# One core, attention and two gated MLPs: the keys' sums read from SBUF, the first DMAs in another order, and P^T v, VectorE's weights work and x pieces moved

## The chip, the cores and the metric

The kernel runs on one core of a Trainium2 chip. The metric is the device time of one execution in microseconds; the median of three runs stands for the kernel. One further execution was recorded by the hardware profiler.

## The reference

Attention with a bias, and behind it two gated MLPs, each on the result of the one before. Four batches, 8 heads, 576 positions, 64 numbers per head; the MLPs see 2304 tokens of 512 numbers with a hidden width of 1536.

```python
scores = q @ k.T / sqrt(64)                       # per head, 576 x 576
cum    = cumsum(maximum(s, 0))                    # s: one number per head and position
scores = where(causal, -1e9, scores + minimum(-(cum[:, None] - cum[None, :]), 0))
attn   = softmax(scores);  x = attn @ v           # heads side by side: 2304 x 512
x = (sigmoid(x @ w_gate) * (x @ w_val)) @ w_out   # first MLP
out = ((x @ w_a) * (x @ w_b)) @ w_out2            # second MLP
```

The six weight matrices arrive in 64-bit floating point.

## The kernel before, in words

**Two parts.** `attention()` works through 32 heads; `mlps()` then runs 1536-wide products in phases over the tokens. TensorE computes with values split into a high and a low half, so each product of the MLPs takes three matmuls (L276 to L278). A weight tile of 512 KB of 64-bit numbers is loaded by SyncE's queue, turned into 32-bit values by one ScalarE (L224) and four VectorE steps (L225, L227, L229, L232), and split by ScalarE (L243) and GpSimd (L244). Nine tiles are treated so during attention (L621), three heads apart; there are three raw buffers and one scratch buffer (`u`, `mag`).

**Order.** In attention every operation has an engine, the operations that it depends on, and a priority; `emit(in_order=True)` (L44) writes out, of the operations whose predecessors are written, always the one with the lowest priority. So each engine's stream, and each DMA queue's, is in the order of priorities, and a waiting instruction holds back all behind it on its engine. One head period is `HT = 6.1`; head i's own time is `t0 = HT * i`. Pools with one buffer each tie steps together: PSUM `g` (row scores), `E` and `F` (transposed scores), `t` (the small transpose and the last piece of the transposed scores), `px` (P^T v).

**A head.** q and k of head i come in by `lqk` (L337). ScalarE rounds them to the high halves (`hq1`, `hk1`, L478 and L479), DMAs copy these to the other 64 partitions (`hk2` on ScalarE's queue L480, `hq2` on SyncE's L481), and VectorE subtracts to get the low halves (`lok` L482, `loq` L484). The bias goes into the same matmul as extra rows: the running sums of s, relative to the start of each quarter (`sums`, L411 to L417, in the SBUF tile `rel`: 128 partitions, quarter by quarter, 32 heads each), and selector rows (`sel`, L385 and L386). For heads 0 to 2 the keys' sums (`relk`, L445) and the queries' sums (`relq`, L423) are copied from `rel` in small DMAs; from head 3 on they come from DRAM (`rel`, L488 and L489), where `relk_d` and `relq_d` were stored by L452, L429 and L454.

TensorE then computes the row scores in two groups, `S(i,0)` and `S(i,1)` (L508, the masks L513), VectorE takes the rows' maxima (`mx`, L521), a small transpose (`mT`, L528), a ScalarE copy (`mc`, L530) and a DMA on ScalarE's queue (`md`, L532) put them into the operand as one more row, and the transposed scores `ST` (L545, L546) come out with the maximum subtracted. ScalarE exponentiates (`ex`, L551), GpSimd masks (`cs`, L567), and `pv` (L582) multiplies with v (`lv`, L341 and L342) in two regions: `pv(i,0)` 256 queries, `pv(i,1)` the rest. ScalarE copies the result out (`xc`, L591), and GpSimd scales it (`xm`, L595) by reciprocals that went through DRAM.

**Order within a period**, on TensorE: `S(i+1,1)`, both regions of `pv(i-2)`, `mT(i+1)`, `S(i+2,0)`, `ST(i)`. At the start, 60 matmuls on a constant (`busy`, L364) run before the first scores; heads 0 to 2 have priorities of their own (`first_at`, L498). The first operand of the MLPs, `xs0`, is prepared during attention in four pieces (`x0h` L628 on ScalarE, `x0l` L629 on VectorE). Two further lines are named below: L205 loads a weight tile, L591 also frees the PSUM that the MLPs' first matmul takes.

Of the kernel before, what the change touches and what calls it, by code (L numbers as in the profile page):

```python
# [7 lines left out]
FP32 = mybir.dt.float32  # L8
# [111 lines left out]
def attn_mlp_kernel(  # L120
# [169 lines left out]
    def attention():  # L290
        with ExitStack() as c2:
# [109 lines left out]

            relk_d = pdr.tile([BH, NR, 2, S], FP32, name="relk_d")
            relq_d = pdr.tile([BH, 3, S], FP32, name="relq_d")
# [51 lines left out]
            relst = ["relk", "relz"] + [("rels", c) for c in range(NR)]  # L455

            HT = 6.1
            NBUSY = 60

# [4 lines left out]
            def head(i):  # L464
# [13 lines left out]
                op(("hq1", i), "ACT", 0.65, lambda: nc.scalar.copy(out=q1[up], in_=r[up]), [("lqk", i)] + done, -251 + 4 * i if i < NR2 else t0 - 3 * HT + 5.2)  # L478
                op(("hk1", i), "ACT", 0.65, lambda: nc.scalar.copy(out=k1[up], in_=r[dn]), [("lqk", i)] + done, -251 + 4 * i if i < NR2 else t0 - 3 * HT + 5.2)  # L479
                op(("hk2", i), "ACT", 0.7, lambda: nc.scalar.dma_start(out=f32(k2[dn]), in_=f32(k1[up])), [("hk1", i)] + done2, -250 + 4 * i if i < NR2 else t0 - 2 * HT + 0.05)  # L480
                op(("hq2", i), "SP", 0.5, lambda: nc.sync.dma_start(out=f32(q2[up]), in_=f32(q1[up])), [("hq1", i)] + done2, -250 + 4 * i if i < NR2 else t0 - 2 * HT + 0.1)  # L481
                op(("lok", i), "DVE", 0.9, lambda: nc.vector.tensor_tensor(  # L482
                    out=k2[up], in0=r[dn], in1=f32(k2[dn]), op=ALU.subtract), [("hk2", i)], -150 + 2 * i if i < 2 else t0 - HT + 3.0)
# [101 lines left out]

                op(("pv", i, 0), "PE", 0.65, lambda: pv(0), [("cs", i, 0), ("lv", i)], t0 + 2 * HT + 0.65, acq=pxk)
                op(("pv", i, 1), "PE", 2.1, lambda: pv(1), [("cs", i, e) for e in range(3)] + [("pv", i, 0)], t0 + 2 * HT + 1.3)
# [33 lines left out]
            for e, key in enumerate(order[:len(early) + NRAW]):  # L621
                split = [4 * HT + 1.6, 4 * HT + 4.6] if e < len(early) else [0, 0]
                weights(sc, *key, [("S", 3 * e - 3, 0)], HT * (3 * e - 2), part=None if e < len(early) else 0,
                        at=[0, 2 * HT + 1.2, 2 * HT + 1.9, 2 * HT + 2.5, 3 * HT + 1.9, 4 * HT + 1.9] + split)

            for k in range(KD):
                t0 = HT * (NH - 12 + k)
                op(("x0h", k), "ACT", 0.4, lambda k=k: nc.scalar.copy(out=xs0[:, 0, k], in_=x_sb[:, k, 0:NB]), [("xm", i) for i in range(H)], t0 + 1.7)  # L628
                op(("x0l", k), "DVE", 0.5, lambda k=k: nc.vector.tensor_tensor(  # L629
                    out=xs0[:, 1, k], in0=x_sb[:, k, 0:NB], in1=f32(xs0[:, 0, k]), op=ALU.subtract), [("x0h", k)], t0 + 2.6)  # L630
            sc.emit(in_order=True)
# [205 lines left out]
```

## Time and profile before

| | |
|---|---|
| time, median of 3 runs | 1130.16 us (1128.74 to 1132.54) |
| the profiled execution | 1131.72 us, its span 1130.0 us, mean granted TensorE clock 0.988 |
| busy, share of the span | TensorE matmul 97%, VectorE 60%, ScalarE 33%, GpSimd 27% |
| bytes moved by DMA | 73.98 MB, mean 65 GB/s |

The page of the profile gives these shares for the whole span. A mean hides stages, so the windows view (busy time of every engine in stretches that one chooses), the waits view (who waited for whom, in total) and the timeline (instructions in order of time) are read for the first 46 us, for the rest of attention (to 236 us) and for the MLPs. A granted clock of 1.00 is 2.4 GHz, 0.50 is 1.2 GHz; between the two a stretch holds both.

### The profile page before, as it was taken

How to read it: one execution, taken by the hardware profiler on the slowest of the kernel's cores; microseconds unless marked ns; L12 is line 12 of the kernel's file. 1: busy time of each engine (PE TensorE's matmuls, PEld its weight loads, DVE VectorE, ACT ScalarE, POOL GpSimd, SP SyncE). 2: the span in 40 equal slices, each digit the busy share in tenths (PEclk: the TensorE clock that was granted, in tenths of full speed). 3: DMA queues.
4: the chain of work that ended last, by engine and by line, in shares of the span. 5: the costliest groups of instructions: out<-in, count | busy, mean ns of one | idle time of the engine just before them, and what ended most of it. 6: DMA issues, size and time to landing. Idle time of an engine off the chain costs nothing.

```text
span 1130.0 us, 14690 instructions
## 1 busy us (share of the span) xinstructions
PE 1100.5 (97%) x5492; PEld 922.7 (82%) x5492; DVE 672.8 (60%) x1004; ACT 370.5 (33%) x614; POOL 304.5 (27%) x343
## 2 busy tenths in 40 slices
PE   5899999999999999999999999999999999999998
PEld 4787777888888888878887888888888888888887
DVE  6688788628248635963596359524953695266333
ACT  2566666544135212421241124324421331132110
POOL 3245645473013201320132013202320232022000
PEclk7799999999999999999999999999999999999999
DMA  4466666533003100310021002101210121000111
GB/s 129 118 179 172 174 157 151 134 93 99 1 2 111 57 1 12 101 56 1 19 94 56 1 19 94 56 1 38 87 45 1 38 93 38 1 19 22 54 38 57
DMA packets 69793, 73.98 MB, mean 65 GB/s; under 512 B 28607, under 2 KB 53367, under 8 KB 69722
## 3 DMA queue, kind: packets, MB, share of 16 engines
q1 hardware_dynamic: 66498, 68.08, 20.9%
q10 hardware_dynamic: 2904, 4.81, 1.8%
q8 instruction: 43, 0.70, 0.3%
q14 instruction: 28, 0.23, 0.1%
q0 software_dynamic: 320, 0.16, 0.1%
HBM read 57.65 MB, written 5.60 MB: 56 GB/s over the span
## 4 chain that ended last, share of the span: by engine, by line
PE 84%; DVE 7%; DMA 4%; issue 2%; POOL 2%; ACT 1%; SPq 0%; ACTq 0%; DVEq 0%; POOLq 0%
PE ps L278 24%; PE ps L277 24%; PE ps L276 24%; PE ps_x L582 5%; PE ps_g L508 2%; DVE raw L229 2%; PE ps_e L545 1%; PE ps_e L546 1%; DVE u L227 1%; DVE raw L232 1%; PE ps_g L513 1%; DMA vx<-in_vm_dram 1%; POOL w L244 1%; DVE nm L521 1%; DMA o<-o 1%
## 5 line engine op out<-in xcount | busy, mean ns | idle before, releaser
L276 PE MATMUL ps<-xs,w 128*128 128x512 f32 (+1 forms) x960 | 353.3, 368 | 0.9 <-ACT xt L591 0.9
L277 PE MATMUL ps<-xs,w 128*128 128x512 f32 (+1 forms) x960 | 353.2, 368 | 0.0
L278 PE MATMUL ps<-xs,w 128*128 128x512 f32 (+1 forms) x960 | 353.1, 368 | 0.0
L726 POOL TENSOR_SCALAR h<-hf 128x512 fp32r<-128x512 f32 (+1 forms) x120 | 90.2, 751 | 515.6 <-DVE hf L715 515.6
L715 DVE TENSOR_TENSOR hf<-ps,g 128x512 f32<-128x512 f32 (+1 forms) x120 | 76.3, 636 | 254.4 <-PE ps L278 253.1
L276 PEld LDWEIGHTS ps<-xs,w 128*128 128x128 f32 x960 | 181.0, 189 | 31.2 <-ACT xt L591 1.0
L277 PEld LDWEIGHTS ps<-xs,w 128*128 128x128 f32 x960 | 181.0, 189 | 30.2
L278 PEld LDWEIGHTS ps<-xs,w 128*128 128x128 f32 x960 | 180.9, 188 | 30.0
L711 ACT ACTIVATE g<-ps 128x512 f32<-128x512 f32 (+1 forms) x120 | 66.5, 554 | 400.5 <-PE ps L278 400.3
L244 POOL TENSOR_TENSOR w<-raw,w 128x512 fp32r<-128x512 f32 x72 | 104.9, 1458 | 176.0 <-ACT w L243 170.9
L729 DVE TENSOR_TENSOR h<-hf,h 128x512 fp32r<-128x512 f32 (+1 forms) x120 | 82.0, 684 | 64.0 <-POOL h L726 64.0
L521 DVE TENSOR_REDUCE nm<-ps_g 128x1 f32<-128x512 f32 (+4 forms) x154 | 73.8, 529 | 38.8 <-PE ps_g L513 38.7
L582 PE MATMUL ps_x<-pt,vx 128*128 128x256 f32 (+1 forms) x434 | 92.6, 365 | 1.4 <-DMA vx<-in_vm_dram 1.2
L278 PE MATMUL ps<-h,w 128*128 128x512 f32 (+1 forms) x240 | 88.5, 369 | 1.5 <-POOL w L244 1.5
L277 PE MATMUL ps<-h,w 128*128 128x512 f32 (+1 forms) x240 | 88.5, 369 | 0.3 <-DVE h L729 0.3
L582 PEld LDWEIGHTS ps_x<-pt,vx 128*128 128x128 f32 x434 | 73.8, 191 | 18.1 <-ACT o L478 1.1
L276 PE MATMUL ps<-h,w 128*128 128x512 f32 (+1 forms) x240 | 88.3, 368 | 0.0
L277 PE MATMUL ps<-w,h 128*128 128x512 f32 x216 | 84.2, 390 | 0.5 <-POOL w L244 0.5
L276 PE MATMUL ps<-w,h 128*128 128x512 f32 x216 | 84.1, 390 | 0.0
L278 PE MATMUL ps<-w,h 128*128 128x512 f32 x216 | 84.0, 389 | 0.0
L567 POOL TENSOR_SCALAR_AFFINE_SELECT pt<-pt 128x256 f32<-128x256 f32 (+1 forms) x96 | 51.1, 554 | 115.1 <-ACT pt L551 109.6
L243 ACT CAST w<-raw 128x512 fp32r<-128x512 f32 x72 | 47.2, 658 | 106.3 <-DVE raw L232 106.2
(100 smaller groups left out, 1398.1 us busy)
## 6 DMA issues: line engine op xcount, KB each, us to landing
raw<-in_moe_w_out_dram SPq DMA_DIRECT2D x24, 512.0 KB
r<-in_qk_dram SPq DMA_DIRECT2D x32, 288.0 KB
raw<-in_moe_w_gate_dram SPq DMA_DIRECT2D x12, 512.0 KB
raw<-in_moe_w_val_dram SPq DMA_DIRECT2D x12, 512.0 KB
raw<-in_moe_w_a_dram SPq DMA_DIRECT2D x12, 512.0 KB
raw<-in_moe_w_b_dram SPq DMA_DIRECT2D x12, 512.0 KB
o<-o SPq DMA_DIRECT2D x32, 144.0 KB
o<-o ACTq DMA_DIRECT2D x32, 144.0 KB
```

Of the source, the lines that this page charges most:

```text
L243: ("ACT", 0.53, lambda: nc.scalar.copy(out=wtile(n, m)[:, 0], in_=value())),
L244: ("Pool", 1.23, lambda: nc.gpsimd.tensor_tensor(out=wtile(n, m)[:, 1], in0=value(), in1=f32(wtile(n, m)[:, 0]), op=ALU.subtract)),
L276: nc.tensor.matmul(out=outp, lhsT=wh, rhs=xh, start=(e == 0), stop=False)
L277: nc.tensor.matmul(out=outp, lhsT=wh, rhs=xl, start=False, stop=False)
L278: nc.tensor.matmul(out=outp, lhsT=wl, rhs=xh, start=False, stop=(e == n - 1))
L521: nc.vector.tensor_reduce(out=nm[0:n, c:c + 1], in_=ps[0:n, p0:p0 + nk], axis=AX.X, op=ALU.max)
L567: nc.gpsimd.affine_select(to, to, [[0, 2], [1, n]][2 - w:], ALU.is_ge, 0.0, base=0, channel_multiplier=-1)
L582: nc.tensor.matmul(out=px[:, 256 + a:256 + q1_], lhsT=vx[:, j], rhs=pt[:, p0:p0 + q1_ - a], start=j == 0, stop=j == js[-1])
L711: op(("g", i, c), "ACT", 0.06 + N * 0.00083, lambda c=c, g=g: nc.scalar.activation(out=sc.get("g", (i, c))[:, 0:N], in_=sc.get("ps", g)[:, ...
L715: op(("hf", i, c), "DVE", 0.07 + N * 0.00104, lambda c=c, u=u: nc.vector.tensor_tensor(out=sc.get("hf", (i, c))[:, 0:N], in0=sc.get("ps", ...
L726: op(("hh", i, c), "Pool", 0.245 + N * 0.00083, lambda c=c, src=src: nc.gpsimd.tensor_scalar(sc.get("h", (i, c))[:, 0, 0:N], src(), 1.0, 1 ...
L729: op(("hl", i, c), "DVE", 0.07 + N * 0.00104, lambda c=c, src=src: nc.vector.tensor_tensor(out=sc.get("h", (i, c))[:, 1, 0:N], in0=src(), ...
```

## The change

- `relk_d` and its store are gone. From head 3 on the keys' sums are copied to the operand straight from `rel` in SBUF (four partitions, two rows of 576 each), in the same place of SyncE's order.
- The first DMAs have another order. `relk` and `relq` of head i stand together at -210 + i, ahead of the copies `hk2` and `hq2`, which move from -250 to about -209; head 2's casts move behind head 0's sums, its selectors from -240 to -220. `relq` goes from ScalarE and GpSimd in turn to: heads 0 and 2 the same two queues, head 1 three on GpSimd's and one on SyncE's. `lok` of heads 0 and 1 moves on VectorE from before the maxima to behind `mx(1,0)` and behind `mx(2,0)`.
- `busy` has 62 matmuls, not 60.
- `pv(i,0)` goes from behind `S(i+3,1)` to in front of it (its priority falls by 0.7; the row scores of that head stand at `t0 + 2 HT`).
- VectorE's weights steps go from the middle of a period (+1.9, +2.5, and +1.9 of the two next) to just before a period's start (-0.15), one period later; the first tile a period later again. The ScalarE and GpSimd splits follow.
- The x pieces go from periods 20 to 23 to periods 27 to 31.

```diff
-            relk_d = pdr.tile([BH, NR, 2, S], FP32, name="relk_d")
...
-                op(("sel", j), ..., (-260, -257, -240, -2)[j], lat=2.2)
+                op(("sel", j), ..., (-260, -257, -220, -2)[j], lat=2.2)
...
-                    name, eng = (("Pool", nc.gpsimd), ("ACT", nc.scalar))[c % 2]
-                    op(("relq", i, c), name, ..., -200 + i, lat=2.2)
+                    name, eng = {"P": ("Pool", nc.gpsimd), "A": ("ACT", nc.scalar), "S": ("SP", nc.sync)}[("APAP", "PPPS", "APAP")[i][c]]
+                    op(("relq", i, c), name, ..., -210 + i + 0.05 * (c + 1), lat=2.2)
...
-            op("relk", "SP", 1.2, lambda: nc.sync.dma_start(
-                out=relk_d.rearrange("b c e s -> c b e s"), in_=f32(rel)), ["sums"], -190, lat=2.5)
...
-            NBUSY = 60
+            NBUSY = 62
+            WLATE = HT
...
-                op(("hq1", i), "ACT", ..., -251 + 4 * i if i < NR2 else t0 - 3 * HT + 5.2)
+                op(("hq1", i), "ACT", ..., (-251, -247, -209.7)[i] if i < NR2 else t0 - 3 * HT + 5.2)
-                op(("hk2", i), "ACT", ..., -250 + 4 * i if i < NR2 else t0 - 2 * HT + 0.05)
+                op(("hk2", i), "ACT", ..., (-209.8, -209.6, -207)[i] if i < NR2 else t0 - 2 * HT + 0.05)
-                op(("hq2", i), "SP", ..., -250 + 4 * i if i < NR2 else t0 - 2 * HT + 0.1)
+                op(("hq2", i), "SP", ..., (-208.5, -207.5, -206)[i] if i < NR2 else t0 - 2 * HT + 0.1)
-                    ... [("hk2", i)], -150 + 2 * i if i < 2 else t0 - HT + 3.0)
+                    ... [("hk2", i)], (-8.7, -8.3)[i] if i < 2 else t0 - HT + 3.0)
...
-                    nc.sync.dma_start(out=f32(k1[D:R1]), in_=relk_d[i].rearrange("c e n -> (c e) n"))
+                    nc.sync.dma_start(out=f32(k1[D:R1]), in_=f32(rel[i:NR * BH:BH]))
...
-                op(("pv", i, 0), "PE", 0.65, ..., t0 + 2 * HT + 0.65, acq=pxk)
+                op(("pv", i, 0), "PE", 0.65, ..., t0 + 2 * HT - 0.05, acq=pxk)
...
-                split = [4 * HT + 1.6, 4 * HT + 4.6] if e < len(early) else [0, 0]
-                weights(sc, *key, ..., HT * (3 * e - 2), ...,
-                        at=[0, 2 * HT + 1.2, 2 * HT + 1.9, 2 * HT + 2.5, 3 * HT + 1.9, 4 * HT + 1.9] + split)
+                split = [5 * HT + 0.2, 5 * HT + 3.2] if e < len(early) else [0, 0]
+                weights(sc, *key, ..., HT * (3 * e - 2) + WLATE * (e == 0), ...,
+                        at=[0, 2 * HT + 1.2, 3 * HT - 0.15, 3 * HT - 0.14, 4 * HT - 0.15, 5 * HT - 0.15] + split)
...
-                t0 = HT * (NH - 12 + k)
+                t0 = HT * (NH - 4 + k)
...
-                ... [("x0h", k)], t0 + 2.6)
+                ... [("x0h", k)], t0 - 0.15)
```

## Rows read from the trace of the kernel before

**Rows 1.** Windows: busy us per engine (count), granted clock, DMA share, GB/s.

```profile
13.14:18.93 5.79, 0.01 (x1) 0.03 (x1) 1.30 (x2) 0.37 (x1) 3.98 (x8) 0.69 0.54 114
18.93:30.90 11.97, 7.25 (x28) 4.90 (x28) 6.09 (x13) 0.51 (x2) 0.00 (x0) 0.50 0.41 120
30.90:37.12 6.22, 4.96 (x18) 3.93 (x19) 3.33 (x6) 3.65 (x6) 1.48 (x3) 0.50 0.61 175
37.12:45.65 8.53, 8.53 (x39) 7.08 (x38) 5.52 (x10) 4.00 (x7) 1.62 (x4) 0.67 0.50 122
100.00:236.00 136.00, 128.61 (x772) 106.53 (x770) 100.06 (x179) 82.17 (x155) 72.92 (x93) 1.00 0.61 149
236.00:1130.00 894.00, 888.07 (x4248) 747.99 (x4248) 501.39 (x687) 237.24 (x367) 194.09 (x191) 1.00 0.14 44
```

**Rows 2.** Waits of TensorE to 44 us: us in total, times, longest.

```profile
PE ps_g L508 <- DMA o<-ya_sb: 6.3, 2, 5.8
...
PE ps_e L545 <- DMA o<-mr: 3.9, 1, 3.9
```

**Rows 3.** Timeline, 0 to 42 us: start, us, engine, line, operation [idle before].

```profile
11.64 3.29 POOL L423 DMA_DIRECT2D o<-ya_sb  x6 [5.57 <-DVE ya_sb L417]
...
14.11 4.73 ACTq L423 DMA_DIRECT2D o<-ya_sb  x6
...
14.37 0.75 DVE L482 TENSOR_TENSOR o<-r,o 64x576 fp32r<-64x576 f32 x1 [0.68 <-DMA o<-o]
...
16.65 2.00 SPq L445 DMA_DIRECT2D o<-ya_sb  x3
...
18.70 0.59 SPq L452 DMA_DIRECT2D relk_d<-ya_sb  x1
...
20.51 1.35 DVE L521 TENSOR_REDUCE nm<-ps_g 128x1 f32<-128x512 f32 x3 [5.39 <-PE ps_g L513]
...
21.78 1.07 DVE L521 TENSOR_REDUCE nm<-ps_x 128x1 f32<-128x256 f32 x2
...
23.18 1.35 SPq L337 DMA_DIRECT2D r<-in_qk_dram  x1
...
32.65 0.67 ACT L478 CAST o<-r 64x576 fp32r<-64x576 f32 x1 [0.32 <-DMA r<-in_qk_dram]
...
33.93 1.01 ACT L551 ACTIVATE pt<-ps_e 128x1024 f32<-128x1024 f32 x1
```

**Rows 4.** Waits of SyncE's queue, 10 to 34 us.

```profile
SPq L488 <- DMA relk_d<-ya_sb: 5.7, 1, 5.7
...
SPq L445 <- DMA o<-o: 1.7, 1, 1.7
```

**Rows 5.** Chain of work that ended last, 13 to 47 us: start, us, what.

```profile
24.14 6.71 DMA o<-mr
```

**Rows 6.** Source view of L423, its DMAs on GpSimd, 0 to 45 us.

```profile
DMA to landing us min/median/max: 2.1/2.6/2.9
```

**Rows 7.** Windows, same columns, 27 to 31 us.

```profile
27.00:31.00 4.00, 0.10 (x1) 0.10 (x1) 1.13 (x3) 0.25 (x1) 0.00 (x0) 0.50 0.25 75
```

**Rows 8.** Waits of TensorE, 44 to 235.9 us.

```profile
PE ps_g L508 <- DVE nm L521: 2.6, 3, 1.5
...
PE ps_g L508 <- DMA o<-relk_d: 1.6, 1, 1.6
...
PE ps_x L582 <- DMA vx<-in_vm_dram: 1.2, 3, 0.6
```

**Rows 9.** Timeline of TensorE in an undisturbed period, 88 to 136 us.

```profile
90.28 0.65 PE L508 MATMUL ps_g<-o 128*128 128x256 f32 x3
...
91.07 2.98 PE L582 MATMUL ps_x<-pt,vx 128*128 128x256 f32 x14
```

**Rows 10.** Timeline, 157 to 176 us: one operation of VectorE, one of GpSimd.

```profile
158.46 1.94 DVE L629 TENSOR_TENSOR xs<-x_sb,xs 128x512 fp32r<-128x512 f32 x1 [0.98 <-ACT xs L628]
...
158.42 1.43 POOL L595 TENSOR_TENSOR x_sb<-xt,rb 64x576 f32<-64x576 f32 x1
```

More of the change, by code (lines that the diff above doesn't have):

```diff
@@ L441, in attention @@
             for j in range(NO):
-                op(("sel", j), "SP", 1.3, lambda j=j: selectors(o_t[j]), ["selc", ("ms", j) if 0 < j < 3 else "more"], (-260, -257, -240, -2)[j], lat=2.2)
+                op(("sel", j), "SP", 1.3, lambda j=j: selectors(o_t[j]), ["selc", ("ms", j) if 0 < j < 3 else "more"], (-260, -257, -220, -2)[j], lat=2.2)
             op("sums", "DVE", 2.7, sums, ["s"], -250)
@@ L477, in head @@
                 op(("lv", i), "SP", 0.9, lambda: load_v(i), [("pv", i - 2, 1), ("sel", 1)], t0 + 4.8, lat=3.0)
[L478 to L481, printed above, removed]
+                op(("hq1", i), "ACT", 0.65, lambda: nc.scalar.copy(out=q1[up], in_=r[up]), [("lqk", i)] + done, (-251, -247, -209.7)[i] if i < NR2 else t0 - 3 * HT + 5.2)
+                op(("hk1", i), "ACT", 0.65, lambda: nc.scalar.copy(out=k1[up], in_=r[dn]), [("lqk", i)] + done, (-251, -247, -209.7)[i] if i < NR2 else t0 - 3 * HT + 5.2)
+                op(("hk2", i), "ACT", 0.7, lambda: nc.scalar.dma_start(out=f32(k2[dn]), in_=f32(k1[up])), [("hk1", i)] + done2, (-209.8, -209.6, -207)[i] if i < NR2 else t0 - 2 * HT + 0.05)
+                op(("hq2", i), "SP", 0.5, lambda: nc.sync.dma_start(out=f32(q2[up]), in_=f32(q1[up])), [("hq1", i)] + done2, (-208.5, -207.5, -206)[i] if i < NR2 else t0 - 2 * HT + 0.1)
                 op(("lok", i), "DVE", 0.9, lambda: nc.vector.tensor_tensor(
-                    out=k2[up], in0=r[dn], in1=f32(k2[dn]), op=ALU.subtract), [("hk2", i)], -150 + 2 * i if i < 2 else t0 - HT + 3.0)
+                    out=k2[up], in0=r[dn], in1=f32(k2[dn]), op=ALU.subtract), [("hk2", i)], (-8.7, -8.3)[i] if i < 2 else t0 - HT + 3.0)
                 op(("loq", i), "DVE", 0.9, lambda: nc.vector.tensor_tensor(
@@ L584, in pv @@
                             start=j == 0, stop=j == js[-1])
-                op(("pv", i, 0), "PE", 0.65, lambda: pv(0), [("cs", i, 0), ("lv", i)], t0 + 2 * HT + 0.65, acq=pxk)
+                op(("pv", i, 0), "PE", 0.65, lambda: pv(0), [("cs", i, 0), ("lv", i)], t0 + 2 * HT - 0.05, acq=pxk)
                 op(("pv", i, 1), "PE", 2.1, lambda: pv(1), [("cs", i, e) for e in range(3)] + [("pv", i, 0)], t0 + 2 * HT + 1.3)
@@ L621, in attention @@
             for e, key in enumerate(order[:len(early) + NRAW]):
-                split = [4 * HT + 1.6, 4 * HT + 4.6] if e < len(early) else [0, 0]
-                weights(sc, *key, [("S", 3 * e - 3, 0)], HT * (3 * e - 2), part=None if e < len(early) else 0,
-                        at=[0, 2 * HT + 1.2, 2 * HT + 1.9, 2 * HT + 2.5, 3 * HT + 1.9, 4 * HT + 1.9] + split)
+                split = [5 * HT + 0.2, 5 * HT + 3.2] if e < len(early) else [0, 0]
+                weights(sc, *key, [("S", 3 * e - 3, 0)], HT * (3 * e - 2) + WLATE * (e == 0), part=None if e < len(early) else 0,
+                        at=[0, 2 * HT + 1.2, 3 * HT - 0.15, 3 * HT - 0.14, 4 * HT - 0.15, 5 * HT - 0.15] + split)
             for k in range(KD):
-                t0 = HT * (NH - 12 + k)
-                op(("x0h", k), "ACT", 0.4, lambda k=k: nc.scalar.copy(out=xs0[:, 0, k], in_=x_sb[:, k, 0:NB]), [("xm", i) for i in range(H)], t0 + 1.7)
+                t0 = HT * (NH - 4 + k)
+                op(("x0h", k), "ACT", 0.4, lambda k=k: nc.scalar.copy(out=xs0[:, 0, k], in_=x_sb[:, k, 0:NB]), [("xm", i) for i in range(H)], t0 - HT + 1.7)
                 op(("x0l", k), "DVE", 0.5, lambda k=k: nc.vector.tensor_tensor(
-                    out=xs0[:, 1, k], in0=x_sb[:, k, 0:NB], in1=f32(xs0[:, 0, k]), op=ALU.subtract), [("x0h", k)], t0 + 2.6)
+                    out=xs0[:, 1, k], in0=x_sb[:, k, 0:NB], in1=f32(xs0[:, 0, k]), op=ALU.subtract), [("x0h", k)], t0 - 0.15)
             sc.emit(in_order=True)
```

4 lines of the change are left out of this document (2 added, 2 removed).

## The prediction

> **What bounds the kernel now.** I read first where TensorE, at 97% of the span, isn't busy, since nothing else can be won. The windows view [rows 1] sorts it by stage. The MLPs, from 236 us on, are busy for 888.07 of 894.00 us: TensorE alone bounds them, and they begin when attention ends. The rest of attention, 100 to 236 us, loses 136.00 - 128.61 = 7.4 us. The start loses most: nothing runs from 13.14 to 18.93 us, 4.7 us are idle from 18.93 to 30.90, and from there to 37.12 another 1.3; nearly all of this runs at the lower granted clock (0.50, 1.2 GHz). The clock fell while TensorE was idle (a mean of 0.69 in a stretch of 5.79 us that holds both levels: 2.2 us after its beginning) and came back in the stretch from 37.12 (mean 0.67, so 5.6 us into uninterrupted work).
>
> Then who ends those waits. TensorE waits 5.8 us in one piece for the last sums of head 0, and 3.9 us for head 0's maxima [rows 2]. The first isn't the sums' computing: GpSimd's copies of them start at 11.64 us, when VectorE is done, but SyncE issues its copies of the keys' sums (L445) only at 16.65 [rows 3], behind a wait of 1.7 us for another copy, o<-o [rows 4]. The second isn't the maxima: their DMA is issued at 24.14 us and lands 6.71 us later [rows 5], against 2.1 to 2.9 us for small copies shortly before [rows 6]. In between, at 18.70, the keys' sums are stored to DRAM [rows 3], and head 3's load from there waits 5.7 us for this store [rows 4]. From 27 to 31 us the DMA engines are busy by 0.25 [rows 7], as much as four of sixteen, and head 3's q and k, issued at 23.18, land only when ScalarE's cast begins, at 32.65 [rows 3].
>
> **The store on four engines: row and skill.** The share of 0.25 [rows 7] says that the tail sits on a quarter of the engines. The Trainium skill, "DMA: Bandwidth & Descriptors", section on why a DMA increments its semaphore by 16, says that a DMA uses the largest number of engines up to 16 that divides the slowest dimension of both sides; the store's is NR = 4, and the trace agrees. The same rule speaks against the new loads of keys' sums: four partitions on one side put them on four engines, where eight rows from DRAM went to eight. By it the one wait of 1.6 us for this load [rows 8] could at most double, and the sum would be 1122.1; on the rows alone it stays.
>
> **The change, part by part.** *To head 0's row scores.* The sums end at about 11.5 us as now. SyncE has its selectors out by then, and the keys' sums go at once instead of at 16.65; GpSimd issues its two of head 0 first (six take 3.29 us [rows 3], so the second is issued by 12.2), ScalarE its two by 13 (six take 4.73). With the median landing of 2.6 us [rows 6] the last arrives at 14.8 (bounds 14.3 with 2.1, 15.9 with ScalarE's last and 2.9). So `S(0,0)` starts at 14.8, not 18.93: **-4.1 us**. The two additional matmuls of `busy` lengthen a run of 60 that is over at 13.14 us by 2/60 of at most 13.14, 0.4 us, and end before 14.8; without that cover they'd cost these 0.4.
>
> *From there to the transposed scores of head 0* (now 11.97 us [rows 1]). With the store gone, `md` lands in 2 to 3 us, and VectorE's line of maxima is what is late next: three reductions of group 0 take 1.35, two of group 1 1.07 [rows 3]. In front of `mT(1)`, which precedes `ST(0)` on TensorE, stand 0.9 of scores, 1.35 + 1.07 + 1.35, then `lok` of head 0 (0.75 [rows 3]), which the change puts there, and 1.07; some 0.4 for transpose and signals: 6.9 us, to 21.7. `md(0)`, issued after the first two maxima at 19.0, lands at 21.6, level with this. **-5.1 us**. Bounds: -3.9 if `md` lands late beside the copies `hk2`, `hq2` and the first weight tile; -6 if it lands in 2 us and the scores are short. The weight load isn't moved on SyncE's queue by its later priority: nothing stands there between -12.2 and -6.1.
>
> *To head 3's row scores* (now 6.22 us). Head 3's q and k may be loaded when `lok(0)` has read the buffer, at 20.3 (now they're issued at 23.18). With 3 us (one more than the smallest landing, for 288 KB) ScalarE casts from 23.3, two times 0.67, then exponentiates 1.01 and two smaller pieces (0.8, from their sizes), with a DMA issue of some 0.6 in between (as the store's [rows 3]). The last piece frees `t` for `mT(2)`, at 27.3, and `S(3,0)` starts at 27.6: 5.9 us, **-0.3**. TensorE has nothing from about 24.5 to 27.3. Bounds: +1.5 if that load lands like the copies queued now, -1 if earlier.
>
> *Head 3 to head 4* (now 8.53 us, its first 5.6 at 1.2 GHz). If the idle 2.8 us drop the clock again, the stretch stays as it is: **0**. If the clock holds, it takes one period, 6.0 (scores, 0.65 + 0.14 for group 1, P^T v 2.98 [rows 9]), with 0.4 for the queues to fill: -2.1. The trace has one comparable row: idle from 13.14 us on, the clock fell within 2.2 us. I take the fall.
>
> *P^T v in front.* `S(i+3,1)` waited three times for VectorE's maxima, 2.6 us in total [rows 8]. The x pieces stood there: one took 1.94 us at 158.46 [rows 10]. Without them in those periods, with the weights steps in the gap before the scores of group 1, and with `pv(i,0)` filling 0.65 us, this goes: **-2.6** (bounds 0 and -2.6). In exchange `pv(i,0)` wants v earlier by the length of group 1, 91.07 - 90.28 = 0.79 us [rows 9], and all behind it on TensorE waits: group 1, its maxima, `mT`. Three heads wait for v already (1.2 us in all [rows 8]); each pays 0.79 more: **+2.4** (bounds 0, if the loads fall otherwise, and 4, if two more heads join).
>
> *The remaining parts cost nothing.* The x pieces at periods 27 to 31 lie where no weights step is left; uncovered, one VectorE piece costs up to 1.94 us before the MLPs. The new load of keys' sums stands in the same place of the queue; the wait of 1.6 us for it [rows 8] stays (bounds: gone, or doubled by four engines). The later weights are needed at 236 us at the earliest.
>
> **The sum** against the profiled execution: -4.1 - 5.1 - 0.3 + 0 - 2.6 + 2.4 = -9.7, so 1131.7 - 9.7 = 1122.0. That execution lies 1.6 above the median of the runs shown; against the median 1130.16 the forecast is 1120.5 us.
>
> **Rivals.** *The clock holds* (chance 0.27): `busy` ends nearer the scores, and the idle stretches are shorter than the 5.79 us of now. It saves the 2.1 above: 1118.4 us. Against it stands the idle stretch before `mT(2)`.
>
> *The start wins half* (0.15): the copies to the other partitions and the first weight tile land together behind the sums, `lok(0)` and head 3's casts wait for them, and ScalarE's stream holds back the exponentials. For it: head 3's casts stand ahead of `ex(0,0)`. With 14.8 kept and 5 us lost again: 1125.5 us.
>
> *VectorE collides with GpSimd* (0.08): the weights steps now stand right before the maxima of group 1. The piece of 1.94 us at 158.46 began beside GpSimd's scaling of x, 1.43 us from 158.42 [rows 10]; doing so in each of nine tiles' three slots, with half of them past the slack before `mT` by 0.4 us, costs 13 x 0.4 = 5: also 1125.5. The Trainium skill, "SBUF — State Buffer", on the shared port pair as an exclusive lock, states such blocking of a VectorE operation with two SBUF inputs by a reading GpSimd one; the long piece fits it, the quick ones beside it don't decide.
>
> *The v loads become the bound* (0.05), the slower side: with `pv(i,0)` first, every head waits for v, because its load follows ScalarE's copy-out on SyncE's queue and can't start earlier. Up to 0.79 us on 29 heads is 23 us: 1130.2 - 9.7 - 2.4 + 23 = 1141. It makes the kernel slower from 12.1 / 29 = 0.4 us per head on. Against it: three waits only among 29 heads now.
>
> *The change is off the path* (0.03): no gain at the start arrives, because the weights of the MLPs set their beginning: 1130. Against it: the first matmul of the MLPs follows attention's last copy, not a weight.
>
> **How the numbers follow.** The forecast has the remaining 0.42 and is the likeliest: 1120.5. Its own range, with the bounds of its terms, is 1117 to 1124.5. The range of 8 in 10 must take in the held clock with the v loads costing nothing (1116) and the two cases at 1125.5: 1115.5 to 1126. A measurement of this kernel tells 0.3%, 3.4 us, from no change, so faster means below 1126.8: all of forecast and held clock, most of the two at 1125.5: 0.86. Within: 0.09, from their rest and the fifth. Slower: 0.05, the v loads.
>
> **What would show it.** `S(0,0)` at 14.3 to 15.9 us; no wait of TensorE over 1 us for md at head 0; `ST(0)` at about 21.7; `S(3,0)` near 27.6, `S(4,0)` near 36 (34 with the clock held), and in the windows a granted clock that falls once after 24 us, or not at all. No TensorE wait on L521 near the x pieces; waits on v of 2 to 4 us in all; MLPs of 894 us as before, begun near 226 us. The prediction is wrong if `md(0)` still takes over 4 us (then the store wasn't its cause), if `mT` waits for VectorE in many periods, or if the time won by 45 us is gone by 236.

## The result and the profile after

The changed kernel takes 1120.45 us (median of four runs, 1117.89 to 1122.1), the kernel before, beside it, 1129.86 us: a ratio of 0.9913, 95% interval 0.9898 to 0.9927. The forecast was 1120.5 us. The profiled execution of the changed kernel is its fastest run (1117.89 us, span 1116.2), 2.6 us below the median; that of before (1131.72) lies 1.9 above the 1129.86. So the two profiles differ by 13.8 us where the medians differ by 9.4, and a stage read from one profile is held below against the other kernels that share the same code.

The line numbers of the changed kernel are one lower than before. First the windows, cut at the same events as [rows 1]: the start to `S(0,0)`, to `ST(0)`, to `S(3,0)`, to `S(4,0)`, a late stretch of attention, the MLPs. Columns: busy us of TensorE's matmuls, its weight loads, VectorE, ScalarE and GpSimd (instructions), granted clock, DMA share, GB/s.

```profile
10.50:13.96 3.46, 3.12 (x29) 2.58 (x28) 1.39 (x2) 0.76 (x2) 3.21 (x6) 1.00 0.12 25
13.96:21.83 7.87, 5.02 (x28) 3.15 (x28) 6.77 (x15) 1.09 (x3) 2.76 (x6) 0.84 0.82 206
21.83:27.98 6.15, 4.89 (x19) 3.92 (x19) 2.79 (x5) 3.57 (x6) 0.99 (x3) 0.65 0.61 168
27.98:33.99 6.01, 6.01 (x39) 5.03 (x38) 5.36 (x10) 3.15 (x6) 1.27 (x3) 1.00 0.85 218
100.00:221.95 121.95, 118.46 (x708) 98.35 (x707) 95.50 (x168) 75.34 (x142) 59.77 (x84) 1.00 0.62 151
221.95:1116.00 894.05, 888.10 (x4248) 748.40 (x4248) 501.09 (x687) 237.12 (x367) 194.31 (x191) 1.00 0.14 44
```

The idle 5.79 us of [rows 1] have shrunk to the 0.34 in front of `S(0,0)`, which starts at 13.96; `ST(0)` starts at 21.83 (before 30.90), `S(4,0)` at 33.99 (before 45.65), the MLPs at 221.95 (before 235.99). The MLPs themselves are as long as they were. The two mixed clocks hold one fall and one rise: 0.84 of 7.87 us is 2.5 us at 1.2 GHz at its end, and 0.65 of 6.15 us is 4.3 at its beginning, 6.8 us together; before, it was from 15.4 to 42.7 us.

The steps in the timeline (start, us, engine, line, operation, idle before and what ended it), in order of time:

```profile
10.47 1.18 SPq L444 DMA_DIRECT2D o<-ya_sb  x2
10.75 3.79 POOL L422 DMA_DIRECT2D o<-ya_sb  x7 [4.69 <-DVE ya_sb L416]
13.96 0.70 PE L507 MATMUL ps_g<-o 128*128 128x512 f32 x3 [0.34 <-ACT o L477]
16.45 0.71 PE L507 MATMUL ps_g<-o 128*128 128x512 f32 x3 [0.91 <-DVE nm L520]
17.88 0.79 ACTq L531 DMA_DIRECT2D o<-mr  x1
20.15 0.35 SPq L337 DMA_DIRECT2D r<-in_qk_dram  x1
21.83 0.80 PE L544 MATMUL ps_e<-o 128*128 128x512 f32 x1 [0.80 <-DMA o<-mr]
23.73 0.67 ACT L477 CAST o<-r 64x576 fp32r<-64x576 f32 x1 [2.41 <-DMA r<-in_qk_dram]
27.74 0.27 PE L527 MATMUL ps_t<-idf,nm 128*5 128x128 f32 x1 [1.26 <-DVE nm L520]
27.98 0.70 PE L507 MATMUL ps_g<-o 128*128 128x512 f32 x3
33.99 0.71 PE L507 MATMUL ps_g<-o 128*128 128x512 f32 x3
```

And TensorE's waits after 44 us (us in total, times, longest), against [rows 8]: the maxima (2.6) are gone, and v costs 2.0 instead of 1.2. A head's sums held it twice before, once for the keys' (1.6) and once for the queries' (0.7, the last line, of the kernel before); now they hold it once, for 1.2.

```profile
PE ps_x L581 <- DMA vx<-in_vm_dram: 2.0, 5, 0.6
PE ps_g L507 <- DMA o<-relq_d: 1.2, 1, 1.2
PE ps L276 <- ACT xt L590: 0.8, 1, 0.8
```

```profile
PE ps_g L508 <- DMA o<-relq_d: 0.7, 1, 0.7
```

### The profile page after: what moved, and what is told of

Its sections match the earlier page's. It is cut to its first block, busy times and chain, and to the rows that moved or that the text cites. A ratio compares the mean times of both kernels' runs of the same rounds, so it can differ in the third digit from the quotient of the medians.

```text
span 1116.2 us, 14691 instructions
## 1 busy us (share of the span) xinstructions
PE 1096.7 (98%) x5494; PEld 920.1 (82%) x5494; DVE 676.7 (61%) x1004; ACT 370.4 (33%) x614; POOL 295.0 (26%) x344
## 4 chain that ended last, share of the span: by engine, by line
PE 83%; DVE 6%; DMA 6%; issue 1%; ACT 1%; POOL 1%; SPq 1%; ACTq 0%; DVEq 0%; POOLq 0%
PE ps L278 24%; PE ps L277 24%; PE ps L276 24%; PE ps_x L581 5%; DMA vx<-in_vm_dram 2%; DVE raw L229 2%; PE ps_g L507 2%; DVE u L227 1%; PE ps_e L544 1%; DVE raw L232 1%; PE ps_e L545 1%; DMA o<-o 1%; PE ps_g L512 1%; POOL w L244 1%; DVE h L728 1%
## 5 line engine op out<-in xcount | busy, mean ns | idle before, releaser
L581 PE MATMUL ps_x<-pt,vx 128*128 128x256 f32 (+1 forms) x434 | 99.6, 370 | 2.1 <-DMA vx<-in_vm_dram 2.0
L581 PEld LDWEIGHTS ps_x<-pt,vx 128*128 128x128 f32 x434 | 76.2, 191 | 19.0 <-ACT o L477 1.5
L566 POOL TENSOR_SCALAR_AFFINE_SELECT pt<-pt 128x256 f32<-128x256 f32 (+1 forms) x96 | 40.5, 440 | 113.3 <-ACT pt L550 112.1
```

The lines of the kernel that those rows point to most:

```text
L566: nc.gpsimd.affine_select(to, to, [[0, 2], [1, n]][2 - w:], ALU.is_ge, 0.0, base=0, channel_multiplier=-1)
L581: nc.tensor.matmul(out=px[:, 256 + a:256 + q1_], lhsT=vx[:, j], rhs=pt[:, p0:p0 + q1_ - a], start=j == 0, stop=j == js[-1])
```

## The experiments

Twelve kernels ran. The kernel before had medians from 1129.35 to 1130.94 us beside them, so they are compared by their ratio to it, each with its 95% interval; 0.001 is 1.1 us. Two events place a profile: `S(4,0)`, the end of the start, and the first matmul of the MLPs.

**The start alone.** P^T v, the weights steps and the x pieces are as before.

```diff
-                op(("pv", i, 0), "PE", ..., t0 + 2 * HT - 0.05, acq=pxk)
+                op(("pv", i, 0), "PE", ..., t0 + 2 * HT + 0.65, acq=pxk)
...
-                weights(sc, *key, ..., HT * (3 * e - 2) + WLATE * (e == 0), ...
+                weights(sc, *key, ..., HT * (3 * e - 2), ...
...
-                t0 = HT * (NH - 4 + k)
+                t0 = HT * (NH - 12 + k)
```

> The changed kernel with P^T v, the weights steps and the x pieces back in their places of before; the store is gone, the first DMAs reordered, 62 matmuls in front. My theory (the start carries the gain): head 4's row scores start at 34 to 36 us against 45.65, and the time is 9 to 11 us under the kernel before; the waits for VectorE's maxima of 2.6 us near the x pieces come back. Rival (the start's gain is lost again before 236 us without the later parts): 5 us or less under the kernel before.

Measured: 0.9930 (0.9909 to 0.9952), 1123.45 us; `S(0,0)` at 15.19, `ST(0)` at 24.65, `S(4,0)` at 38.53. That is less than the theory (34 to 36 us, and 9 to 11 us under the kernel before): the medians lie 6.8 us apart. TensorE waits 3.6 us for the maxima later on, as it said. By the ratios the start carries four fifths of the gain (0.0070 of 0.0087).

**The later parts alone**, in the kernel before: the same three edits the other way.

```diff
-                op(("pv", i, 0), "PE", ..., t0 + 2 * HT + 0.65, acq=pxk)
+                op(("pv", i, 0), "PE", ..., t0 + 2 * HT - 0.05, acq=pxk)
...
-                t0 = HT * (NH - 12 + k)
+                t0 = HT * (NH - 4 + k)
```

> The kernel before with P^T v in front, the weights steps and the x pieces as in the changed kernel, and the start untouched. My theory: the waits for maxima (2.6 us) go, the waits for v grow by up to 2.4; the time is 0 to 2.6 us under the kernel before. Rival (most of the gain sits here): 5 us or more under it. Slower rival: the waits for v grow by over 3 us, and the kernel is slower than before.

Measured: 0.9983 (0.9968 to 0.9997), 1128.43 us, 1.8 us under the kernel before beside it, as the theory says. The waits for the maxima are gone, v costs 1.2 us over two heads.

**No store**, in the kernel before: the keys' sums come from SBUF, the order of the first DMAs stays.

```diff
...
-            op("relk", "SP", 1.2, lambda: nc.sync.dma_start(
-                out=relk_d.rearrange("b c e s -> c b e s"), in_=f32(rel)), ["sums"], -190, lat=2.5)
...
-                    nc.sync.dma_start(out=f32(k1[D:R1]), in_=relk_d[i].rearrange("c e n -> (c e) n"))
+                    nc.sync.dma_start(out=f32(k1[D:R1]), in_=f32(rel[i:NR * BH:BH]))
```

> One edit to the kernel before: no store of the keys' sums, the loads from head 3 on read SBUF. My theory (the store alone holds up head 0's maxima and head 3's operands): the DMA of head 0's maxima lands in 2 to 4 us instead of 6.7, the transposed scores of head 0 start at 26.5 to 28 us instead of 30.9, head 0's row scores stay at 18.9; 3.5 to 5.5 us under the kernel before. Rival (the weight load of 512 KB issued beside it holds them up): the DMA still takes over 5 us and the time changes by under 1 us.

Measured: 0.9977 (0.9962 to 0.9993), 1128.24 us. `md(0)` lands 3.97 us after its issue instead of 6.71 [rows 5], TensorE's wait for it falls from 3.9 us [rows 2] to 1.2, and `ST(0)` comes at 27.86 instead of 30.90, but `S(4,0)` only at 42.47, and the medians lie 2.0 us apart: the mechanism held, the gain was smaller than the 3.5 to 5.5 us expected.

**The store in another layout**, in the kernel before: 128 rows outermost (4 quarters of 32 heads) instead of 4 quarters.

```diff
-            relk_d = pdr.tile([BH, NR, 2, S], FP32, name="relk_d")
+            relk_d = pdr.tile([NR * BH, 2, S], FP32, name="relk_d")
...
-                out=relk_d.rearrange("b c e s -> c b e s"), in_=f32(rel)), ["sums"], -190, lat=2.5)
+                out=relk_d, in_=f32(rel)), ["sums"], -190, lat=2.5)
...
-                    nc.sync.dma_start(out=f32(k1[D:R1]), in_=relk_d[i].rearrange("c e n -> (c e) n"))
+                    nc.sync.dma_start(out=f32(k1[D:R1]), in_=relk_d[i:NR * BH:BH])
```

> One edit to the kernel before: the store stays, with the same bytes, but its outer dimension is 128 partitions instead of 4, so that all sixteen engines may share it; the loads from DRAM read it in that layout. If it is the four engines that make it late: landing in 3 to 5 us instead of 11.5, no stretch at a DMA share of 0.25 from 27 to 31 us, and nearly the gain of the kernel without the store (3 to 5 us under the kernel before). If it is the bytes or the write to DRAM: landing above 8 us and under 1 us gained.

Measured: 0.9980 (0.9966 to 0.9995), 1127.74 us: 2.5 us under the kernel before, a little less than expected and about what leaving the store out gives. The store lands 3.6 us after its issue instead of 11.55. In the waits view of SyncE's queue, the 5.7 us of [rows 4] that head 3's load waits for the store become

```profile
SPq L488 <- DMA relk_d<-ya_sb: 0.2, 1, 0.2
```

The bytes are the same; the outermost dimension of the copy differs, and with it the order of the rows in DRAM. That it is the four engines shows in the trace of the kernel before. It holds a landing mark for each of a load's parts, and head 3's q and k have sixteen: twelve are in by 27.07 us, the other four come at 30.36, 30.52, 31.69 and 32.63, each 2.3 to 2.4 us behind one of the store's four (27.98, 28.14, 29.41 and 30.24). With the store in the other layout all sixteen are in by 24.73. So a quarter of the engines held up the store, and with it a part of every load queued behind it, as the prediction read from [rows 7]. The rule of the Trainium skill cited there ("DMA: Bandwidth & Descriptors", the section on why a DMA increments its semaphore by 16) agrees.

**The changed kernel with the store**, in its old layout: the new order, without the new source.

```diff
...
+            op("relk", "SP", 1.2, lambda: nc.sync.dma_start(
+                out=relk_d.rearrange("b c e s -> c b e s"), in_=f32(rel)), ["sums"], -190, lat=2.5)
...
-                    nc.sync.dma_start(out=f32(k1[D:R1]), in_=f32(rel[i:NR * BH:BH]))
+                    nc.sync.dma_start(out=f32(k1[D:R1]), in_=relk_d[i].rearrange("c e n -> (c e) n"))
```

> The changed kernel with its new order of loads, but the head's keys' sums are stored to memory and loaded from there again, as before. Theory (the new order and the missing store are two separate savings that meet at the dynamic mask's first load): S(0,0) still starts at 14 to 15 us, but the first mask load is issued beside the store and lands at about 26 to 28 us, so ST(0) starts at about 28 instead of 21.8 us, S(4,0) comes 2 to 5 us later than in the changed kernel, and the time is 1123 to 1127 us. Rival (the order alone carries the gain): ST(0) stays within 1 us of 21.8 and the time stays at 1120 to 1121.5 us.

Measured: 0.9988 (0.9977 to 0.9999), 1127.56 us. Nearly all of the gain is gone, more than expected, although `S(0,0)` starts at 14.82. Three rows of its timeline:

```profile
26.25 0.79 PE L547 MATMUL ps_e<-o 128*128 128x512 f32 x1 [4.48 <-DMA o<-mr]
32.94 0.67 ACT L480 CAST o<-r 64x576 fp32r<-64x576 f32 x1 [10.87 <-DMA r<-in_qk_dram]
35.86 0.38 PE L530 MATMUL ps_t<-idf,nm 128*5 128x128 f32 x1 [4.89 <-DMA vx<-in_vt_dram]
```

`md(0)`, issued at 18.73 beside the store, lands at 26.21. Worse is the second row: head 3's q and k, issued at 23.73, land at 32.92, and ScalarE waits 10.87 us for them with a cast; the exponentials of head 0 stand behind that cast. The third row's releaser is misread by the view (that load lands at 36.98, later than the matmul): `mT(2)` needs the buffer `t`, which the last exponential reads until 35.81. `S(4,0)` comes at 43.66, two microseconds before [rows 1]'s 45.65.

**The changed kernel with the store in the other layout.**

```diff
...
+            op("relk", "SP", 1.2, lambda: nc.sync.dma_start(
+                out=relk_d, in_=f32(rel)), ["sums"], -190, lat=2.5)
...
-                    nc.sync.dma_start(out=f32(k1[D:R1]), in_=f32(rel[i:NR * BH:BH]))
+                    nc.sync.dma_start(out=f32(k1[D:R1]), in_=relk_d[i:NR * BH:BH])
```

> The changed kernel with the keys' sums stored and loaded again, but stored as 96 rows of one layout, the form that landed in 3.6 instead of 11.5 us when it was put into the kernel before. Theory (the store's slowness on four DMA engines, not the round trip, is what cost 7 us when it was put back): the store lands in 3 to 5 us, the raw rows that ScalarE waited 10.9 us for land before 26 us, S(4,0) is within 2.5 us of the changed kernel's 34.0, and the time is 1120.5 to 1123 us. Rival (the round trip, its bytes and its place on the queue cost as much in any form): 1125 to 1128 us.

(The rows are 128, not 96.) Measured: 0.9951 (0.9932 to 0.9969), 1126.59 us median, though its profiled execution took 1121.65. The store lands in 4.8 us, q and k of head 3 at 25.86, `S(4,0)` at 36.40: in the profile the theory holds, but the median lies in the rival's range, and half of what was lost stays lost. So by ratio the store costs 0.0075 in the new order, of which 0.0037 is its layout and 0.0038 the round trip itself, where it was 0.0023 in the old order (no store) in all. Each of the two parts is uncertain by about 0.002.

**P^T v back behind the scores.**

```diff
-                op(("pv", i, 0), "PE", ..., t0 + 2 * HT - 0.05, acq=pxk)
+                op(("pv", i, 0), "PE", ..., t0 + 2 * HT + 0.65, acq=pxk)
```

> The changed kernel with P^T v's first part put back behind the row scores' group 1. Theory (the maxima waits went with the x pieces and weights steps, and the part of P^T v in front only brings the wait for the v loads earlier): TensorE's wait for v loads falls from 2.0 us to between 0 and 1.2, the maxima waits stay under 1 us in all, the time is 1118.5 to 1120.5 us. Rival (the part of P^T v in front is what removed the waits for the maxima): 2 to 3 us of such waits come back and the time is about 1122 to 1123.5 us.

Measured: 0.9918 (0.9906 to 0.9931), 1119.62 us. The waits for v are gone, 2.6 us of waits for the maxima are back (the theory had said under 1; this part is as the rival says), and the time is that of the changed kernel all the same: a swap of one wait for another of about the same size.

**The x pieces back.**

```diff
-                t0 = HT * (NH - 4 + k)
+                t0 = HT * (NH - 12 + k)
```

> The changed kernel with the eight x pieces put back to the batches where they stood before, on ScalarE and VectorE. Theory (they held up the maxima): TensorE's waits for the maxima in the last third of the attention come back with 1 to 3 us and the time is 1121.5 to 1123.5 us. Rival (the other two moves are enough): no wait for the maxima over 0.5 us in all, 1120 to 1121 us.

Measured: 0.9923 (0.9910 to 0.9936), 1120.74 us, waits for the maxima of 0.4 us. The theory fell: with P^T v in front, the x pieces do not hold up the maxima.

**VectorE's weights steps back.**

```diff
-                split = [5 * HT + 0.2, 5 * HT + 3.2] if e < len(early) else [0, 0]
-                weights(sc, *key, ..., HT * (3 * e - 2) + WLATE * (e == 0), ...
-                        at=[0, 2 * HT + 1.2, 3 * HT - 0.15, 3 * HT - 0.14, 4 * HT - 0.15, 5 * HT - 0.15] + split)
+                split = [4 * HT + 1.6, 4 * HT + 4.6] if e < len(early) else [0, 0]
+                weights(sc, *key, ..., HT * (3 * e - 2), ...
+                        at=[0, 2 * HT + 1.2, 2 * HT + 1.9, 2 * HT + 2.5, 3 * HT + 1.9, 4 * HT + 1.9] + split)
```

> The changed kernel with VectorE's weights steps (and the first weight's steps that WLATE delays) put back to where they stood before. Theory (neither the x pieces nor the part of P^T v brought the maxima waits back when they were put back, so these steps were what held up the maxima): TensorE's waits for the maxima between 45 and 222 us come back with 1.5 to 3 us, and the time is 1121.5 to 1123.5 us. Rival (any two of the three moves are enough): under 1 us of such waits, 1120 to 1121 us.

Measured: 0.9968 (0.9956 to 0.9981), 1127.51 us: 6 us of the gain are lost, three times what the theory said, and not through the maxima (0.2 us). TensorE's waits from 45 us to the MLPs name another:

```profile
PE ps_x L581 <- ACT xt L590: 5.6, 12, 0.5
```

P^T v of a head waits, in twelve heads, for ScalarE's copy of the result of the head before. One such period, all engines:

```profile
125.33 2.26 POOL L566 TENSOR_SCALAR_AFFINE_SELECT pt<-pt 128x256 f32<-128x256 f32 x3 [2.93 <-ACT pt L550]
125.77 0.84 DVE L229 SCALAR_TENSOR_TENSOR raw<-raw,u 128x512 int32<-128x512 int32 x1
126.64 0.85 DVE L481 TENSOR_TENSOR o<-r,o 64x576 fp32r<-64x576 f32 x1
127.67 1.44 POOL L594 TENSOR_TENSOR x_sb<-xt,rb 64x576 f32<-64x576 f32 x1
129.14 0.64 ACT L590 COPY xt<-ps_x 128x576 f32<-128x576 f32 x1 [1.85 <-POOL x_sb L594]
129.83 0.92 PE L581 MATMUL ps_x<-pt,vx 128*128 128x256 f32 x4 [0.50 <-ACT xt L590]
```

From bottom to top: P^T v waits for the copy, the copy for GpSimd's scaling (L594, which frees the copy's target), the scaling stands behind GpSimd's three mask pieces (L566), and these take 2.26 us while VectorE runs a weights step (L229) and `lok` (L481) beside them. The changed kernel at the same place:

```profile
125.54 0.64 DVE L229 SCALAR_TENSOR_TENSOR raw<-raw,u 128x512 int32<-128x512 int32 x1
125.75 1.24 POOL L566 TENSOR_SCALAR_AFFINE_SELECT pt<-pt 128x256 f32<-128x256 f32 x3 [3.24 <-ACT pt L550]
126.96 1.42 POOL L594 TENSOR_TENSOR x_sb<-xt,rb 64x576 f32<-64x576 f32 x1
127.19 1.80 DVE L481 TENSOR_TENSOR o<-r,o 64x576 fp32r<-64x576 f32 x1
```

The mask pieces take 1.24 us, and now `lok` is the longer one, beside the scaling. The groups of GpSimd's masks from 45 to 222 us (xcount | busy us, mean ns of one | idle before; the mean mixes pieces of 128x256 with a smaller one of 64x64), of the kernel before, the changed kernel and this experiment:

```profile
L567 POOL TENSOR_SCALAR_AFFINE_SELECT pt<-pt 128x256 f32<-128x256 f32 (+1 forms) x84 | 46.1, 572 | 85.7 <-ACT pt L551 80.2 <-PE ps_g L513 4.7 <-POOL pt L567 0.2
```

```profile
L566 POOL TENSOR_SCALAR_AFFINE_SELECT pt<-pt 128x256 f32<-128x256 f32 (+1 forms) x87 | 36.6, 439 | 93.9 <-ACT pt L550 93.0
```

```profile
L566 POOL TENSOR_SCALAR_AFFINE_SELECT pt<-pt 128x256 f32<-128x256 f32 (+1 forms) x82 | 50.0, 630 | 81.9 <-ACT pt L550 78.5 <-PE ps_g L512 3.0
```

**The start and the weights steps**, without the other two moves (the edits of P^T v and of the x pieces above, together).

```diff
+                op(("pv", i, 0), "PE", ..., t0 + 2 * HT + 0.65, acq=pxk)
...
+                t0 = HT * (NH - 12 + k)
```

> The change without two of its parts: the start and VectorE's weights steps as in the changed kernel, P^T v's first part and the x pieces as before. Theory (VectorE's weights steps used to run beside GpSimd's masks and lengthen them, 572 ns a piece before, 630 with the weights steps put back, 439 in the changed kernel; moving these steps carries all that the later parts bring): the masks take 430 to 460 ns a piece, ScalarE's copies out of P^T v wait for GpSimd under 20 us in all, TensorE waits for the maxima under 1.5 us, and the time relative to the kernel before is 0.990 to 0.9925, as in the changed kernel. Rival (the weights move only repairs what P^T v in front would cost, and by itself brings nothing): 0.993, as with the start alone, with 3 us or more of waits for the maxima.

Measured: 0.9928 (0.9906 to 0.9950), 1122.16 us. The masks take 430 ns a piece and the copies wait 14.7 us for GpSimd, as the theory says; but the waits for the maxima are 3.9 us, as the rival says, and the time lies between the two and doesn't decide. The moves' worth can be read only in combination: the weights steps' place is worth 6 us with P^T v in front, and nothing measurable without (0.9928 against the start alone, 0.9930). The other way round, P^T v in front and the late x pieces without the weights move (0.9968) lose 4 us against the start alone.

**TensorE's gaps filled.** 35 matmuls on constants that nothing reads, in the gaps of the changed kernel's start.

```diff
...
+            for n, at in ((8, -8.89), (2, -8.71), (6, -8.55), (3, -8.41), (6, 4.1), (10, 9.45)):
+                op(("fill", at), "PE", 0.1 * n, fill(n, ("fill", at)), ["mkb"] + ([("ex", 0, 1)] if at > 5 else []) + [("S", 0, 1)], at, ...)
```

> The changed kernel with 35 matmuls that nothing reads put into TensorE's idle gaps between S(0,1) and mT(2) of the first batch; nothing else moves. Theory (about a third of a microsecond of time goes with each microsecond that TensorE spends at its lower clock level, and the clock falls because of those gaps): the granted clock stays at its upper level from S(0,0) on or falls for under 2 us in place of 6.8 in the profile and 9.0 in the mean of the runs, and the time falls by 1 to 3 us to 1117.5 to 1119.5 us. Rival (the start is bound by loads and by VectorE alone, the clock only follows): the clock is held and the time stays within 0.7 us of 1120.4. Second rival: the fillers stand in front of due matmuls and the time rises by up to 2 us.

Measured: 0.9929 (0.9910 to 0.9949), 1120.95 us. The runs spend 4.9 us at the lower clock in the mean (from each run's mean clock; 9.0 in the changed kernel's), yet nothing is won: the time is the first rival's. The last ten fillers waited 2.1 us for the exponentials that free their buffer and ran 1.25 us in front of `mT(2)`, which came at 28.76 instead of 27.74.

**Only the first 25 fillers**, and P^T v behind (the edit of P^T v above, and against the kernel with all fillers).

```diff
-            for n, at in ((8, -8.89), (2, -8.71), (6, -8.55), (3, -8.41), (6, 4.1), (10, 9.45)):
+            for n, at in ((8, -8.89), (2, -8.71), (6, -8.55), (3, -8.41), (6, 4.1)):
```

> The changed kernel with the first 25 of the 35 filling matmuls (those before mT(2), which waited for the exponentials and ran 1.25 us in front of it, are left out) and with P^T v's first part behind the row scores' group 1. Theory (the lower clock level costs time by itself): at most 5 us at the lower level in the mean of the runs, S(3,0) at 28.0 us or earlier, and 1118 to 1119.3 us, 0.5 to 2 us under the changed kernel. Rival (the clock level of the start only goes with the loads' lateness, and the loads set the time): the same 1119.5 to 1121 us as with all fillers.

Measured: 0.9928 (0.9909 to 0.9948), 1122.68 us; 4.9 us at the lower clock in the mean. The theory fell; the median lies above the rival's range too. The kernel with P^T v behind and no fillers is the one to hold this against (0.9918, its clock low from 19.59 to 26.42 us). With the fillers the clock holds in that stretch, and `S(3,0)`, at 27.81, comes 13.18 us after `S(0,0)` instead of 14.04. That is only 0.86 us sooner, because another path then ends last: head 3's q and k, its casts and the exponentials, for which `mT(2)` waits:

```profile
27.60 0.38 PE L527 MATMUL ps_t<-idf,nm 128*5 128x128 f32 x1 [2.10 <-ACT pt L550]
```

And the clock falls all the same, later, in the period from `S(3,0)` to `S(4,0)`, where TensorE has no gap. That stretch in the kernel with the x pieces back and in this one, against 6.01 us in the changed kernel (at 1.00) and in the one with P^T v behind:

```profile
29.64:37.24 7.60, 7.60 (x38) 6.43 (x38) 5.67 (x10) 3.22 (x6) 1.00 (x3) 0.78 0.45 108
```

```profile
27.81:36.52 8.71, 8.71 (x39) 7.27 (x38) 5.06 (x9) 3.64 (x7) 1.48 (x5) 0.65 0.71 172
```

0.78 of 7.60 us is 3.3 us at 1.2 GHz and costs 1.6; 0.65 of 8.71 is 6.1 and costs 2.7: somewhat under half a microsecond for each, where TensorE is busy throughout. In the changed kernel's profile the lower clock lay from 19.35 to 26.17 us, in stages whose ends are set by `md(0)` and by VectorE's maxima, with waits of 0.80 and 1.26 us at these ends. In that gappy start 6.8 us at the lower clock cost 0.86, about an eighth of a microsecond for each. The fillers did not avoid the fall, they moved it on, in this profile into a stretch that TensorE alone bounds.

## Why the prediction was right

The order of the waits, their causes in the main and the gain came out as forecast: 9.4 us by the medians, where 9.7 were summed. That the median hits 1120.5 to 0.1 us is luck, since several steps are off and partly cancel, and one was right by a wrong cause. Profile against profile:

| step | forecast | profile | what it was |
|---|---|---|---|
| to `S(0,0)` | -4.1 | -5.0 | 13.96 us; 14.43, 14.64, 14.77, 14.84 and 15.19 in the other five profiles with this start, no store and no fillers |
| to `ST(0)` | -5.1 | -4.1 | `md(0)` took 3.9 us, not 2 to 3 |
| to `S(3,0)` | -0.3 | -0.1 | set by the maxima, not by head 3's load |
| to `S(4,0)` | 0 | -2.5 | the clock was back |
| rest of attention | -2.6 + 2.4 | -2.4 | maxima as forecast, v less, the sums' loads 1.1 less |
| MLPs | 0 | +0.2 | 894.25 against 894.01 us |

**To `S(0,0)`** the step held. The profile's extra 0.9 us is not the change's: the load of s, for which VectorE's sums wait, landed at 6.65 us, in the other five at 7.13 to 7.88 (GpSimd's copies start at 10.75 us, against 11.64 in [rows 3]), and in all six `S(0,0)` starts 3.2 us after the first of these copies. The view puts the end of its wait to a cast of ScalarE for head 2, on which it doesn't depend; by the trace's landing marks, the last of head 0's sums, issued by ScalarE at 11.96 us, landed at 13.61. The six starts together have a median of 14.7 us, where 14.8 was forecast.

**To `ST(0)`** the path was named rightly, but its end was `md(0)`, level with the maxima in the forecast: issued at 17.88 us, a microsecond earlier than thought, it landed 3.9 us later, and TensorE waits 0.80 us for it. The result, -4.1, is near the bound of -3.9 that stood for an `md` that lands late. The reason given there, the copies and the first weight tile beside it, isn't shown: without the store, in the old order, `md(0)` takes 3.97 us too, issued at 23.84, when the weight tile has landed (22.11). In the other five profiles with this start it takes 3.88 to 4.85 us, in three of them over 4, which is the prediction's own sign that the store wasn't the cause. The runs with and without the store put it in between, since the store caused a part of the landing: 2.7 of 6.71 us in the old order (3.97 without it), 3.6 of 7.48 in the new (3.91 without it). That a small copy lands here in 2 to 3 us without the store was wrong.

**To `S(3,0)`** the time was right and the cause wrong. Head 3's q and k were cast from 23.73 us (forecast 23.3), but the last exponential freed `t` at 26.66, not 27.3; what ended last was VectorE's maxima of `S(2,1)`, a group that TensorE ran at the lower clock. In the other four profiles with this start and the weights steps or P^T v moved, or the x pieces back, `S(3,0)` comes at 28.47 to 29.64 us, and in the start alone at 30.87, later than the forecast's 27.6.

**To `S(4,0)`** the forecast let the clock fall in the idle stretch after 24 us and charged it to this stretch. In the profile it fell at 19.35, in the gaps between the first scores, was back at 26.17, and the stretch took 6.01 us, the held-clock rival's time (6.0 and 0.4). Which of the two happens differs between executions: 7.60 us with the x pieces back, whose start is the same code. `S(4,0)` came at 33.99, 34.48, 36.27, 36.52 and 37.24 us in these five and at 38.53 in the start alone, on both sides of the forecast's 36.15; the profiled run is the earliest and the fastest; the others of the changed kernel have no profile. What was measured is thus probably a mixture of the forecast and that rival. The sum against the profiled run (1122.0) missed its 1117.89 by 4.1 us: 2.5 for the clock, 2.2 for the rest of attention and 0.9 for the early sums, less 1.4 for later steps that came out slower.

**Rest of attention.** The maxima's 2.6 us went, as forecast, but of the three moves that it gave as causes one suffices. With P^T v in front these waits are 0 to 0.4 us in every kernel (the x pieces or the weights steps back included), with P^T v behind 1.7 to 3.9; there the late x pieces make 1.3 us of difference (2.6 against 3.9, one profile each). v pays 0.8 us more, not 2.4: five heads wait, two more than before, as the upper bound allowed, but each shortly. The waits for the loads of a head's sums, which the forecast let stand, fell from 2.3 us in two to 1.2 in one; but the same loads cost 2.8 us in four waits in the kernel before without its store, and with the x pieces back this one among others:

```profile
PE ps_g L507 <- DMA o<-ya_sb: 2.4, 1, 2.4
```

So whether the doubling that the prediction worked out from the rule of the Trainium skill ("DMA: Bandwidth & Descriptors", the section on why a DMA increments its semaphore by 16) happens there isn't decided. The x pieces' later dates cost nothing measurable, as forecast. The weights steps' move, to which the sum gave no price of its own, is worth 6 us beside P^T v in front.

**The rivals.** VectorE's collision with GpSimd was seen with the wrong sign: the old place of the weights steps is the colliding one, and the price of 5 us that stood for the new place is what the old one costs (6 us) once P^T v stands in front. The mechanism of the start that wins half, casts of head 3 that hold back the exponentials, is what the changed kernel with the store in it shows; there it takes nearly the whole gain. The v loads as the bound and the gain off the path are refuted: 2.0 us of waits, and what is won by `S(4,0)` (11.7 us) is still there at the MLPs (14.0).

**What the forecast did not see** is that the two halves of the start need each other. It added -4.1 for the order and -5.1 for the store as if each stood alone. By ratio the store's removal alone gives 0.0023; the new order with the store gives nothing beyond the later parts (0.9988 against their 0.9983); both give 0.0070. The first wait hides the second: with the order alone the store is issued just when `md(0)` and head 3's q and k must go out.

Open are three things: what besides the store keeps `md(0)` at 3.9 us and more; why the round trip in the fast layout still costs 0.0038 in the median, since its profiled execution is the fastest of its six runs and shows little of it; and what P^T v in front brings at all, since its two halves cancel within the intervals.

## What to carry to other kernels

Where two waits follow each other on one path, price the edits together as well as apart: removing either one here gave a third of what both gave, or nothing. A step that moves one engine's work is judged by who runs beside it at the new place and at the old one, and the price may appear three engines away. Before filling gaps to keep TensorE's clock up, see where the clock would fall instead: each microsecond at the lower level cost about an eighth of one in the start with its gaps, almost half of one in a stretch that TensorE alone bounds.

## What the runs showed of the hardware

A GpSimd mask piece of 128x256 takes 0.41 us when no two-input VectorE operation runs beside it, and 0.64 to 0.75 us when one does (medians of 17 to 39 pieces from 45 to 222 us in the kernels before, changed, and with the weights steps back); spans on GpSimd are rough, but ScalarE's copy and P^T v move with them. The reverse holds too: `lok` takes 0.75 us alone [rows 3] and 1.80 or 2.02 beside GpSimd's scaling. The Trainium skill, "SBUF — State Buffer", section "SBUF: two separate sides", says that a VectorE operation with two SBUF inputs and a GpSimd operation that reads SBUF exclude each other for the whole instruction; `lok` at 121.10 us in the changed kernel agrees, since it takes 2.02 us beside a scaling of 1.43 us that began 0.02 us earlier, about the one after the other (1.43 + 0.75 = 2.18). Where `lok` began first, at 146.60 us, it took 0.75 us and the scaling 2.02.

The layout of one store of 576 KB changed its landing from 11.55 to 3.6 us, and what it delayed was not only its reader: copies of 2.5 KB (`md`) and of 288 KB (q and k) issued while it was under way took 7.5 and 9.2 us from issue to landing in the changed kernel with the old store, 3.9 and 3.6 us without it.
